# The up-projection's moving operand is read from its last column to its first, and its tiles are laid out 4128 bytes apart

## The chip, the cores and the metric

The kernel runs on one core of a Trainium2 chip. A core has a matrix engine (TensorE, PE in the profile, with its weight loads as PEld), a vector engine (VectorE, DVE), a scalar engine (ScalarE, ACT), a general engine (GpSimd, POOL) and an engine that here only issues DMAs (SyncE, SP). SBUF is the working memory of 128 partitions, PSUM holds the matmul results in eight banks. Times are device microseconds of one execution. The kernel before takes 2546.99 us, the median of 2 runs (2546.63 and 2547.34).

## The reference

```python
x = A_x                                               # 2 x 1 x 4096 x 640
g = _sigmoid((x * gate_w).sum(-1, keepdims=True))
a = _A_ref(x, A_w1, A_b1, A_w2, A_b2)
b = _B_ref(x, B_w_gate, B_w_up, B_w_down)
return g * a + (1 - g) * b

# _B_ref: (gelu(x @ w_gate) * (x @ w_up)) @ w_down, with 640 -> 1728 -> 640
# _A_ref: rfft over the 4096 tokens; in four blocks of 160 channels a complex two-layer MLP
#         (relu between), soft threshold at 0.01; irfft
```

There are 8192 tokens of 640 channels. The largest part is branch B, two projections of 640 to 1728 columns (w_gate and w_up, together the "up-projection" here) and one back.

## The kernel before, in words

All matrix products are built from a high and a low part. A float32 operand is split into a rounded part (ScalarE, `high`, L276) and the rest (VectorE, `low`, L279), both of type float32r, and a product is three matmuls: high times high, high times low, low times high. Each matmul has one weight load (LDWEIGHTS) of 128 columns of its own, so PE and PEld have equal counts.

The kernel has three stages:

1. The up-projection, from the start to about 1388 us. It goes through 16 blocks of 512 tokens, three times, once for each of three groups of hidden columns. The hidden layer h is written to DRAM (`h_store`). Beside it, ScalarE, VectorE and a few matmuls (L619) compute the gate and the first step of the Fourier transform.
2. The spectral MLP of branch A, to about 1812 us: the second step of the transform (L783), two layers (L295, L860 to L863), the first step back.
3. The down-projection together with the last step of the inverse transform, to the end.

In stage 1 the tokens are the moving operand (tiles xo, 256 tokens a matmul, streamed through the array) and the projection weights the stationary one (tiles w0 to w3). `quad` multiplies two 2x2 blocked matrices with seven products instead of eight, so the tokens enter as sums and differences of blocks, named b11, b21, b12, b22, k4 and t1 to t5. Each name is one tile xo of [128 partitions, 2 parts, 512 tokens]; t5 holds 256 tokens. `x_of` cuts from these tiles the pieces of 256 columns that the matmuls read. A quad runs 54 matmuls in seven runs: of 9, 9, 6, 9, 9, 6 and 6, each run over one tile or two. `plain` (first block of the first group) runs 60 matmuls without the seven-product form, `mixed` (the last 64 gate and 64 up columns, once a block in the third group) 30. All matmuls of this stage and of the down-projection are issued in `run`, so they stand under one line, L472, and are told apart by their tiles: xo and w here, wx and ho in the down-projection.

The tiles xo come from the pool tag "mid", which has 14 slots, each as large as the largest mid tile. The other users of mid are of the later stages (z, zz, zl, h, hs, s2s and the down-projection's wx in part). Before the first mid tile the helper `mid` allocates two small tiles named gap and clears them on POOL (L239): one in a "tiny" slot, one of 112 words in a tag of its own, which sets where the mid slots begin. As the program is built, the mid slots stand at 171,712 + 4096k bytes within each partition, so each starts 64 bytes past a multiple of 128. The tiles of the other pools that TensorE reads (w0, w1, w2 and ho in "big", w3 in "tiny", xs in "small") start at multiples of 128.

The tokens reach xo in two ways. In the first group each xo is made from the raw tokens (xraw, loaded by SP from in_xT), and t1 to t4 are also written to DRAM (xD, by POOL's queue). In the other groups t1 to t4 are loaded back ready split, 124 loads by SP's queue. Nothing is put in order by a planner: the program writes each engine's order out by hand (hooks at numbered points of each quad, and lists of due loads).

The host lays out the inputs before the launch: `_layouts` permutes and reshapes, among them the array xT from which xraw is loaded.

Of the kernel before, what the change touches and what calls it, by code (L numbers as in the profile page):

```python
# [10 lines left out]
F32 = mybir.dt.float32  # L11
# [4 lines left out]
P = 128  # L16
# [134 lines left out]
def _tokens():  # L151

    n2, q = np.arange(32)[:, None], NB[None, :]
    return np.where(n2 < 16, 32 * q + n2, 32 * (P - 1 - q) + n2)


def _layouts(a):

    A = lambda n: np.asarray(a[n])
    c = np.ascontiguousarray  # L160
    x = A("A_x")[:, 0]
    even, odd = np.arange(BS), np.roll(np.arange(BS), -32)
    main = np.concatenate([n * BS + (odd if n % 2 else even)[:P] for n in range(NBLK)])
    rest = np.concatenate([n * BS + (odd if n % 2 else even)[P:] for n in range(NBLK)])
    perm = np.concatenate([main, rest])
    xt = x[:, _tokens()]
    o = {"x": c(xt[..., perm]), "gate": c(A("gate_w")[perm][None])}

    xp = xt.reshape(16, 2, 256, 5, P).transpose(0, 4, 1, 3, 2)
    o["xT"] = c(np.stack([xp[:, :, 0, :2], xp[:, :, 0, 2:4], xp[:, :, 1, :2], xp[:, :, 1, 2:4], xp[:, :, :, 4]],  # L170
                         axis=1).reshape(16, 5, P, 512))

    g, u = A("B_w_gate"), A("B_w_up")
    cols = []
    for t in range(NPAIR):
        cols += [g[:, t * P:(t + 1) * P], u[:, t * P:(t + 1) * P]]
    cols.append(np.concatenate([g[:, NPAIR * P:], u[:, NPAIR * P:]], axis=1))
    o["wgu"] = c(np.stack([m.reshape(5, P, P).transpose(1, 0, 2) for m in cols]))
    o["wd"] = c(A("B_w_down"))

    w1, w2 = A("A_w1"), A("A_w2")
    w1 = np.stack([w1[:, n][:, odd if n % 2 else even] for n in range(NBLK)], axis=1)
    b1, b2 = A("A_b1")[:, :, None], A("A_b2")[:, :, None]

    def wide1(w):
        m, r = w[..., :P], w[..., P:]
        return np.concatenate([m[1], r[1], r[0], r[1], m[0], m[1]], axis=-1)

    def wide2(w):
        return np.concatenate([w[1], w[0], w[1]], axis=-1)  # L190

    def long1(w):
        m, r = w[..., :P], w[..., P:]
        return np.concatenate([m[0], m[1], r[0], r[1]], axis=-1)

    def long2(w):
        return np.concatenate([w[0], w[1]], axis=-1)

    def rows(w, f, order):
        return np.stack([f(w[[z, 1 - z], :, i]) for z, i in order])  # L200
    i32 = range(P, BS)
    tr = lambda w: c(w.transpose(1, 0, 2))
    o["w1m"], o["w2m"] = tr(wide1(w1[:, :, :P])), tr(wide2(w2[:, :, :P]))
    o["w1l"] = c(rows(w1, long1, [(z, i) for i in i32 for h in range(2) for z in range(2)]))
    o["w2l"] = c(rows(w2, long2, [(z, i) for h in range(2) for z in range(2) for i in i32]))
    o["w1s"] = c(np.concatenate([rows(w1, long1, [(z, i) for i in i32 for z in range(2)]),
                                 tr(long1(b1)).repeat(2, 0)]))
    o["w2s"] = c(np.concatenate([rows(w2, long2, [(z, i) for z in range(2) for i in i32]),
                                 tr(long2(b2)).repeat(2, 0)]))
    return o  # L210
# [3 lines left out]
def spectral_mix_kernel(ctx: ExitStack, tc: tile.TileContext, a):  # L214
# [7 lines left out]
    pool = ctx.enter_context(tc.tile_pool(name="pool", bufs=1))  # L222
# [7 lines left out]
    gap = []  # L230
# [3 lines left out]

    def mid(shape, dt=F32, name="mid"):
        if not gap:
            gap.extend([tiny([P, 1], name="gap"), pool.tile([P, 112], F32, name="gap", tag="gap", bufs=1)])
            for t in gap:
                nc.gpsimd.memset(t, 0.0)  # L239
        return pool.tile(shape, dt, name=name, tag="mid", bufs=14)  # L240
# [4 lines left out]
    def tiny(shape, dt=F32, name="tiny"):  # L245
        return pool.tile(shape, dt, name=name, tag="tiny", bufs=15)
# [168 lines left out]
    def x_prep(key, k, eng=nc.vector):  # L415
# [4 lines left out]
        def src():  # L420
            d = XT[key]
            if not made(key) and kept is not None:
                m = mid([P, 2, 512], F32R, name="xo")
                ld(m.rearrange("p h n -> p (h n)").bitcast(F32), xD[key[1]][:, kept])
                XO.setdefault(key, {})[name] = [m[:, h] for h in range(2)]
                return
            for n, p, q in (("t1", "b12", "b11"), ("t2", "b22", "t1"), ("t3", "b22", "b12"), ("t4", "b21", "t2")):
                if n not in d and (n == name or (n, name) == ("t1", "t2")):
                    d[n] = small([P, 512], name="xd")
                    nc.vector.tensor_sub(d[n], d[p], d[q])  # L430
            if name == "t5":
                d[name] = small([P, 256], name="xd")
                nc.vector.tensor_sub(d[name], d["k4"][:, :256], d["k4"][:, 256:])
            return d[name]

        def hi():
            if not made(key) and kept is not None:
                return
            if name == "t5":
                if not T5:  # L440
                    T5.append(mid([P, 2, 2, 256], F32R, name="xo"))
                t = [T5[0][:, keys.index(key) % 2, h] for h in range(2)]
            else:
                m = mid([P, 2, 512], F32R, name="xo")
                t = [m[:, h] for h in range(2)]
                if kept is not None:
                    XM[key, name] = m
            XO.setdefault(key, {})[name] = t
            high(t[0], XT[key][name])
# [30 lines left out]
    def x_of(o, *names):  # L480

        tiles = []
        for n in names:
            n, q = n if isinstance(n, tuple) else (n, None)
            h, l = o[n]
            for k in ((0,) if n == "t5" else (0, 1) if q is None else (q,)):
                tiles.append((h[:, 256 * k:256 * k + 256], l[:, 256 * k:256 * k + 256]))
        return tiles

    Q = []  # L490
# [1 line left out]
    def quad(key, t, hook):  # L492
# [8 lines left out]

        X = half()
        run(X, prod(w["g1"], x_of(o, "b11", ("k4", 0))))
        p1 = T("p1")
        copy(p1, X)
        hook(0)
        old[0]()
        hook(1)
        C = half()
        run(C, prod(w["s3"], x_of(o, "t3", ("k4", 1))))  # L510
        hook(2)
        A = half()
        run(A, prod(w["g2"], x_of(o, "b21")))
        nc.vector.tensor_add(p1, A, p1)  # L514
        hook(3)
# [961 lines left out]
```

## Time and profile before

| | before |
|---|---|
| median of the runs | 2546.99 us |
| lowest and highest run | 2546.63, 2547.34 us |
| profiled execution, first to last instruction (span) | 2546.4 us |
| TensorE busy | 2535.1 us of the span |
| weight loads busy | 2530.4 us |
| VectorE, ScalarE, GpSimd busy | 2055.1, 1502.8, 370.2 us |
| instructions | 54296 |

The profiled execution's span ends 0.6 us under the median of the runs. In a row of a group, the name left of the arrow is what is written and those right of it are what is read, then come the shape and the count; behind the first bar the group's busy time in us and the mean length of one instruction in ns; behind the second the engine's idle time ahead of it and whom it waited for. Matmuls overlap each other in the array, so their mean length is longer than the distance at which they follow each other. That distance comes from the chain of work that ended last, listed in order of time: each row is a start, a length (both in us) and a count of instructions that followed each other without a gap.

### The profile page before, as it was taken

The numbers are of one execution on the slowest core, as the hardware profiler recorded it, in microseconds if no ns is written. First come the engines' busy times: TensorE is split into PE (matmuls) and PEld (weight loads), VectorE is DVE, ScalarE is ACT, GpSimd is POOL, SyncE is SP. The second block draws the span as 40 slices with busy tenths as digits, with TensorE's granted clock in tenths as the row PEclk, the third lists the DMA queues.
The fourth block names the chain that finished last, engine by engine and source line by source line (L and its number), as shares of the span: only waits on it lengthen the run. The fifth ranks groups of instructions, "written<-read, shape, count | busy, mean of one in ns | idle before, by whom it ended". The sixth has DMA issues, their size and how long they took to land.

```text
span 2546.4 us, 54296 instructions
## 1 busy us (share of the span) xinstructions
PE 2535.1 (100%) x20276; PEld 2530.4 (99%) x20276; DVE 2055.1 (81%) x4212; ACT 1502.8 (59%) x3490; POOL 370.2 (15%) x370
## 2 busy tenths in 40 slices
PE   9999999999999999999999999999999999999999
PEld 9999999999999999999999999999999999999999
DVE  7778777777777766776667788888899999999998
ACT  6555555666665655555556777778644444445443
POOL 0000000000000000000002111111133333333332
PEclk9999999999999999999999999999999999999999
DMA  6565657676767667776667455548844444344442
GB/s 232 190 215 196 212 170 234 205 236 211 219 205 249 207 213 231 224 230 214 212 222 223 129 153 150 160 137 266 291 149 138 150 156 158 120 144 156 155 136 92
DMA packets 346060, 483.48 MB, mean 190 GB/s; under 512 B 24701, under 2 KB 222717, under 8 KB 345797
## 3 DMA queue, kind: packets, MB, share of 16 engines
q1 hardware_dynamic: 331108, 438.47, 54.5%
q0 software_dynamic: 14688, 41.56, 4.5%
q8 instruction: 159, 2.61, 0.4%
q14 instruction: 105, 0.85, 0.1%
HBM read 300.29 MB, written 179.64 MB: 188 GB/s over the span
## 4 chain that ended last, share of the span: by engine, by line
PE 97%; DMA 1%; DVE 1%; issue 0%; ACT 0%; SPq 0%; DVEq 0%; ACTq 0%
PE bank L472 77%; PE bank L295 14%; PE bank L783 3%; PE bank L619 1%; DMA wx<-wdf 1%; PE bank L861 1%; PE bank L860 1%; DMA wx<-wdl 0%; PE bank L863 0%; DVE xo L279 0%; DMA wraw<-in_wgu_dram 0%; DVE xd L430 0%; DVE h L543 0%; DVE w L279 0%; DVE wl L715 0%
## 5 line engine op out<-in xcount | busy, mean ns | idle before, releaser
L472 PE MATMUL bank<-xo,w 128*128 128x256 f32 x11736 | 1362.0, 277 | 6.3 <-ACT xo L276 5.1
L472 PEld LDWEIGHTS bank<-xo,w 128*128 128x128 f32 x11736 | 1353.0, 188 | 7.5 <-ACT xo L276 5.1
L472 PE MATMUL bank<-wx,ho 128*128 128x320 f32 x4608 | 678.6, 308 | 0.1
L472 PEld LDWEIGHTS bank<-wx,ho 128*128 128x128 f32 x4608 | 674.1, 188 | 0.6 <-DMA wx<-wdf 0.3
L498 ACT ACTIVATE u<-bank 128x256 f32<-128x256 f32 x408 | 156.7, 384 | 258.0 <-PE bank L472 252.5
L279 DVE TENSOR_TENSOR ho<-hraw,ho 128x640 fp32r<-128x640 f32 (+3 forms) x384 | 276.9, 761 | 5.0 <-ACT ho L276 3.0
L276 ACT ACTIVATE ho<-hraw 128x640 fp32r<-128x640 f32 x320 | 166.3, 574 | 64.1 <-PE bank L472 46.8
L498 ACT ACTIVATE p<-bank 128x256 f32<-128x256 f32 x204 | 78.6, 385 | 149.0 <-PE bank L472 66.4
L279 DVE TENSOR_TENSOR xo<-xraw,xo 128x512 fp32r<-128x512 f32 x209 | 142.9, 684 | 25.2 <-ACT xo L276 24.7
L531 DVE TENSOR_TENSOR u<-bank,u 128x256 f32<-128x256 f32 x204 | 85.9, 421 | 90.8 <-ACT u L498 88.2
L279 DVE TENSOR_TENSOR xs<-xr,xs 64x640 fp32r<-64x640 f32 x128 | 105.0, 820 | 58.0 <-ACT xs L276 56.0
L1165 ACT ACTIVATE uu<-bank,gs 128x320 f32<-128x320 f32 x120 | 55.0, 525 | 160.0 <-PE bank L295 157.7
L295 PE MATMUL bank<-wm,h 128*128 128x320 f32 (+1 forms) x792 | 137.8, 309 | 0.0
L540 DVE TENSOR_TENSOR u<-bank,u 128x256 f32<-128x256 f32 x204 | 85.5, 419 | 62.2 <-PE bank L472 61.3
L276 ACT ACTIVATE xo<-xraw 128x512 fp32r<-128x512 f32 x209 | 131.0, 627 | 7.1 <-DMA xraw<-in_xT_dram 5.3
L621 DVE TENSOR_TENSOR as<-bank,as 64x320 f32<-64x320 f32 x256 | 113.9, 484 | 25.0 <-ACT as L620 24.0
L295 PEld LDWEIGHTS bank<-wm,h 128*128 128x128 f32 (+1 forms) x792 | 118.6, 185 | 1.2
L276 ACT ACTIVATE ho<-hs 128x640 fp32r<-128x640 f32 (+1 forms) x128 | 71.9, 576 | 77.8 <-PE bank L472 57.7
L572 POOL MEMSET h<- 64x512 f32 x16 | 8.4, 522 | 747.7 <-PE bank L619 369.4
L514 DVE TENSOR_TENSOR p<-bank,p 128x256 f32<-128x256 f32 x204 | 86.5, 424 | 36.6 <-PE bank L472 32.2
L279 DVE TENSOR_TENSOR s2s<-s,s2s 128x320 fp32r<-128x320 f32 x128 | 111.6, 929 | 0.9 <-ACT s2s L276 0.9
L620 ACT ACTIVATE as<-bank 64x320 f32<-64x320 f32 x256 | 96.8, 427 | 16.5 <-PE bank L619 14.0
(157 smaller groups left out, 3470.7 us busy)
## 6 DMA issues: line engine op xcount, KB each, us to landing
xo<-xD SPq DMA_DIRECT2D x124, 512.0 KB
xraw<-in_xT_dram SPq DMA_DIRECT2D x225, 256.0 KB
hD<-h SPq DMA_DIRECT2D x224, 256.0 KB
hraw<-hD SPq DMA_DIRECT2D x128, 320.0 KB
xD<-xo POOLq DMA_DIRECT2D x64, 512.0 KB, 4.4
sc<-scr SPq DMA_DIRECT2D x65, 320.0 KB
xr<-in_x_dram SPq DMA_DIRECT2D x64, 320.0 KB
scr<-as SPq DMA_DIRECT2D x64, 320.0 KB
```

What stands on the lines that cost most here:

```text
L276: nc.scalar.activation(dst, src, AF.Copy, scale=scale)
L279: eng.tensor_sub(dst, src, hi.bitcast(F32))
L295: nc.tensor.matmul(dst, l, r, start=i == 0, stop=i == len(ops) - 1)
L472: nc.tensor.matmul(dst, l, r, start=first and i == 0, stop=i == len(ops) - 1, skip_group_check=True)
L498: copy = lambda d, s_: nc.scalar.activation(d, s_, AF.Copy)
L514: nc.vector.tensor_add(p1, A, p1)
L531: nc.vector.tensor_add(u4, C, u4)
L540: nc.vector.tensor_add(u2, C, u2)
L620: nc.scalar.activation(stg[hi, cs], pa[lo, :320], AF.Copy)
L621: nc.vector.tensor_add(stg[hi, cs], pa[hi, :320], stg[hi, cs])
L783: nc.tensor.matmul(pz[:, kp * P:(kp + 1) * P], SC[b, c, kp][:, o:o + P], ft, start=True, stop=True)
L1165: nc.scalar.activation(uu[n2][:, cs], pe[:, :320], AF.Copy, scale=gs[:, b, 0, n2:n2 + 1])
```

## The change

Three edits. On the host, the last axis of the array behind xT, the 256 tokens of a half block, is turned round. In `x_of`, both parts of each piece of 256 columns are handed to the matmul with step -1, from the last column to the first; the product in PSUM therefore has the order of before. In `mid`, the gap tile of 112 words in its own tag becomes one of 1032 words in the tag mid; since 1032 words are more than any other mid tile has (1024), the slots become 4128 bytes long. As the program is built they stand at 171,264 + 4128k, that is 0, 32, 64, 96, 0, ... bytes past a multiple of 128, fourteen different starts modulo 4096. The whole of the memory used is the same, and so is the order of the instructions on PE, DVE, ACT and SP; on POOL one memset is longer. Two tiles, the split of an xd and one load of xo, now also carry a wait for POOL's memset, as the first users of the slot after the gap tile.

```diff
@@ _layouts
-    xp = xt.reshape(16, 2, 256, 5, P).transpose(0, 4, 1, 3, 2)
+    xp = xt.reshape(16, 2, 256, 5, P).transpose(0, 4, 1, 3, 2)[..., ::-1]
@@ mid
-            gap.extend([tiny([P, 1], name="gap"), pool.tile([P, 112], F32, name="gap", tag="gap", bufs=1)])
+            gap.extend([tiny([P, 1], name="gap"), pool.tile([P, 1032], F32, name="gap", tag="mid", bufs=14)])
             for t in gap:
                 nc.gpsimd.memset(t, 0.0)
@@ x_of
-                tiles.append((h[:, 256 * k:256 * k + 256], l[:, 256 * k:256 * k + 256]))
+                tiles.append(tuple(x[:, 256 * k:256 * k + 256][:, ::-1] for x in (h, l)))
```

## The prediction

> **What bounds the kernel now.** I read the page's busy line first, then the granted clock, then the chain that ended last, and last the groups by line and shape. The clock comes from the view of cores, the rest from the page and from the list of groups of TensorE.
>
> ```profile
> span 2546.4 us, 54296 instructions
> PE 2535.1 (100%) x20276; PEld 2530.4 (99%) x20276; DVE 2055.1 (81%) x4212; ACT 1502.8 (59%) x3490; POOL 370.2 (15%) x370
> q1 hardware_dynamic: 331108, 438.47, 54.5%
> PE 97%; DMA 1%; DVE 1%; issue 0%; ACT 0%; SPq 0%; DVEq 0%; ACTq 0%
> ```
>
> ```profile
> core 0: 2546.4 us, clock 1.000
> L472 PE MATMUL bank<-xo,w 128*128 128x256 f32 x11736 | 1362.0, 277 | 6.3 <-ACT xo L276 5.1 <-ACT u L498 0.9 <-DVE xo L279 0.4
> L472 PE MATMUL bank<-wx,ho 128*128 128x320 f32 x4608 | 678.6, 308 | 0.1
> L295 PE MATMUL bank<-z,wm 128*128 128x256 f32 x360 | 62.2, 281 | 0.0
> L239 POOL MEMSET gap<- x2: 99/146/192, 0.7 to 0.8; 128x1 f32 x1, 128x112 f32 x1
> ```
>
> TensorE ends last for 97% of the span, and for the up-projection (the 11,736 matmuls that read xo) it stood idle 6.3 us in all. So the time is the number of matmuls times the spacing at which they start. The mean of 277 ns is the length of one pipelined matmul and not that spacing. The spacing is seen in the chain listed in order of time, in which an unbroken run of matmuls is one row (start, length, count):
>
> ```profile
> 6.03 3.67 PE bank L472 x16
> ...
> 66.91 22.38 PE bank L472 x190
> 89.29 0.29 PE bank L619 x2
> ```
>
> ```profile
> 243.56 21.56 PE bank L472 x190
> 290.22 0.29 PE bank L619 x2
> 290.51 2.97 PE bank L472 x26
> 293.77 74.95 PE bank L472 x661
> 1352.21 0.89 PE bank L783 x8
> 1858.52 21.02 PE bank L472 x144
> ```
>
> Four things are to be seen. (a) The long undisturbed row gives 74.95/661 = 113.4 ns for one matmul of 256 columns. (b) The same work with the same tiles ran in another rhythm at 66.9 us: 22.38/190 = 117.8 ns, 4.4 ns more each, through the whole row. The shapes and the pools it reads from are the same, so the spacing isn't fixed by the column count alone. (c) L619 reads a tile of another pool (xs), which starts at a multiple of 128 bytes, while every xo tile of before starts 64 bytes past one (the built program puts the mid slots at 171,712 + 4096k). After those two matmuls the next row is dearer: 2.97 us for 26 where 26 x 113.4 ns = 2.95, so 22 ns more; and 21.56 us for 190 where 21.54 is due, 16 ns more. A visit to a tile of another class and back costs the next few matmuls about 19 ns, then the old rhythm returns. (d) At 128 columns a row of L783 takes 0.89/8 = 111 ns a matmul, hardly less than at 256 columns: there the weight load, one for each matmul, sets the pace.
>
> **The change, part by part.** No instruction is added, removed or moved on PE, DVE, ACT or SP; the order by engine is the same in both programs. Three things change.
>
> First, the gap tile of 112 words in its own slot becomes one of 1032 words in a mid slot. The one clearing instruction that grows on POOL took at most 192 ns for 112 words; nine times that is 1.7 us, and by its row POOL had begun it at 0.8 us. Its only followers are a split on ACT and one xo load in SP's queue that reuse this slot some thirteen mid tiles later; the memset is over long before. Cost 0. If a wait did go to it, it would be once, under 2 us.
>
> Second, the widest mid tile is now 4128 bytes instead of 4096, so the fourteen slots lie 4128 apart, from 171,264 on: 0, 32, 64 or 96 bytes past a multiple of 128 in turn (four, four, three and three slots). Before, all fourteen were alike. The pool takes 14 x 32 = 448 = 112 x 4 bytes more and the gap gives those back; every other pool stays where it was.
>
> Third, each of the 11,736 matmuls of the up-projection reads its 256 columns with step -1 from offset 255. The host has reversed the tokens, so the products and PSUM are as before, and the splits and DMAs still write forward. What DVE, ACT and DMA do has slack: ACT 59% busy, DVE 81%, the hardware queue 54.5% of the engines' time. That the 124 loads of xo now land on 32-byte starts is therefore hidden unless they become so slow that TensorE, which waited 6.3 us in all, begins to wait for them.
>
> What the step of -1 costs has no row: no matmul of before reads backwards. The bounds per matmul:
> - below nothing: down to the 111.3 ns of L783, -2.1 ns, 11,736 x -2.1 = -25 us;
> - nothing: the rhythm of 113.4 ns holds, 0;
> - the other rhythm, 117.8 ns: 11,736 x 4.4 = 52 us;
> - far above: columns streamed at half the rate. The row at 6.03 us, the kernel's first matmuls, which ran at about half the later pace, stands nearest: 3.67/16 = 229 ns, +116 ns each, 11,736 x 116 = +1,360 us.
>
> [...]
>
> I take the step itself at nothing, and price the classes. The nearest row for those is (c), a tile of another class. One quadruple product runs 54 matmuls over 11 xo tiles in turn (seven runs, four of them over two tiles); 204 of those, 4 plain blocks with 12 turns each and 16 mixed ones with 6 make 204 x 11 + 48 + 96 = 2,388 changes of tile. Before, none changed class. Now two different slots share a class with chance (4x3 + 4x3 + 3x2 + 3x2)/(14x13) = 0.20, so about 1,910 changes do. At 19 ns each: 36 us. For bounds: 0 if only the direction relative to the weights counts, and 2,388 x 22 ns = 53 us if all pay the dearer price. A step of 32 bytes has no row; I price it as the one of 64.
>
> The other readers of mid slots still read forward: the z matmuls (62.2 us), a few groups of its kind, and some 960 of the 4,608 down-projection matmuls, whose weights lie in mid slots. The row of these is 21.02/144 = 146.0 ns; 320 columns at the pace of (a) would be 141.7. So +/-4.3 ns on 960 is +/-4 us, and as much again for the z groups: 0 taken, +/-8 us kept.
>
> Sum against the profiled execution: 2546.4 + 36 = 2582.4 us of span. The median of the runs is 0.6 us above that span, so 2583 us, 1.4% slower. A measurement of this kernel can tell 2% (51 us) from no change: the borders are 2496 and 2598.
>
> **The rivals.**
>
> *The change is invisible* (it doesn't do what it says, as far as time goes): the spacing stays at 113.4 ns and the time at 2540 to 2555. For it: (a) holds for 661 matmuls that go through many tiles, at distances of many slots. Against it: (b) and (c), the same matmul at two spacings.
> [...]
>
> *A better rhythm.* Reading backwards pairs differently with the weight load, and the spacing falls to the load's own pace of 111.3 ns: -25 us, 2521. For it: that pace exists. Against it: 113.4 was reached with all tiles in one class, and now four classes must all lock. It can't gain 2%, as the load floor stops it.
>
> *A worse rhythm, on the slow side.* Place: each start of a moving stream in the up-projection. Mechanism: with changing classes the good rhythm of (a) never re-forms and everything runs as in (b), 52 us, while each change of class still pays, 36 us: 2546.4 + 88 = 2634. It decides from 117.8 ns on average: more than 51 us over 11,736 matmuls is 4.4 ns each. If half of all matmuls paid the 22 ns of (c), 129 us, it would be 2675. For it: row (b) shows that a rhythm once lost can stay lost for 190 matmuls. Against: in all later rows it came back after a few.
>
> *The stream runs at half rate backwards:* +1,360 us, 3,900. [...] Then ACT and DVE would idle before PSUM results, and nothing else would move.
>
> **How the numbers follow.** Forecast (classes cost, the direction doesn't), 2555 to 2597: 0.44. Invisible, 2540 to 2555: 0.13. Better rhythm, 2515 to 2540: 0.07. Worse rhythm, 2597 to 2680: 0.19, of it 0.18 past 2598. Half rate, about 3,900: 0.14. Anything else, 0.03: 0.02 faster than 2496, 0.01 between 2680 and 3,900. The range from 2515 to 2680 leaves out 0.17. Faster by over 2%: 0.02; within 2%: 0.44 + 0.13 + 0.07 + 0.01 = 0.65; slower: 0.18 + 0.14 + 0.01 = 0.33. Within the forecast's own case the time is 2555 to 2597.
>
> **What the profile of the changed kernel would show.** If I am right, the chain's long rows of L472 stand at 115.5 to 117 ns a matmul (76.3 to 77.3 us for the row of 661), with no row as clean as 113.4; the group of xo matmuls is busy some 1,398 us; the rows of L619 and the two stages behind the up-projection keep their length within 10 us. Half rate shows at once as 2,700 us busy in that group. The invisible case keeps the row of 661 at 74.95. The worse rhythm shows rows near 120 ns. I am wrong in kind if xo matmuls begin to wait for loads (their idle time far above 6.3 us), or if the down-projection, which still reads forward, takes the difference.

## The result and the profile after

The changed kernel takes 2604.14 us, the median of 2 runs (2603.86 and 2604.41), against 2546.99 us: the ratio is 1.0218 with a 95% interval from 1.0201 to 1.0234, so it is 2.2% slower.

First lines of the changed kernel's page, then the gap tile's row from the view of its line, and the clock from the view of cores.

```profile
span 2602.1 us, 54297 instructions
PE 2590.7 (100%) x20276; PEld 2586.6 (99%) x20276; DVE 2062.6 (79%) x4212; ACT 1505.0 (58%) x3490; POOL 374.0 (14%) x370
...
L472 PE MATMUL bank<-xo,w 128*128 128x256 f32 x11736 | 1414.6, 282 | 6.2 <-ACT xo L276 5.2
L472 PE MATMUL bank<-wx,ho 128*128 128x320 f32 x4608 | 680.0, 309 | 0.3 <-DVE ho L279 0.3
L239 POOL MEMSET gap<- x2: 99/528/958, 0.7 to 0.8; 128x1 f32 x1, 128x1032 f32 x1
core 0: 2602.1 us, clock 1.000
```

The span grew by 55.7 us, and the xo matmuls are busy 1414.6 us instead of 1362.0, 52.6 us more. Their idle time is 6.2 us against 6.3: no new wait for loads or splits came up. The clock is the same. The memset of the gap tile takes 0.96 us and holds nobody up.

Where the time went in the stages is read from the first and last start of the two groups under L472. The view of that line gives them, of before and then of after (duration as minimum, median and maximum in ns, then first and last start in us):

```profile
L472 PE MATMUL bank<-xo,w x11736: 276/276/583, 5.1 to 1386.3; 128*128 128x256 f32 x199
L472 PE MATMUL bank<-wx,ho x4608: 302/309/414, 1812.1 to 2541.6; 128*128 128x320 f32 x192
```

```profile
L472 PE MATMUL bank<-xo,w x11736: 278/282/582, 5.2 to 1438.5; 128*128 128x256 f32 x199
L472 PE MATMUL bank<-wx,ho x4608: 302/309/417, 1865.8 to 2597.3; 128*128 128x320 f32 x192
```

The up-projection ends 52.2 us later. The MLP stage between (1812.1 - 1386.3 = 425.8 us before, 1865.8 - 1438.5 = 427.3 after) grew by 1.5 us and the last stage by 2.0 us. So the loss is in the matmuls that the change touches. The chain in order of time shows at which spacing:

```profile
226.44 22.53 PE bank L472 x190
248.98 0.29 PE bank L619 x2
249.27 3.07 PE bank L472 x26
...
305.02 150.58 PE bank L472 x1270
...
1935.33 21.09 PE bank L472 x144
```

The longest run gives 150.58/1270 = 118.6 ns a matmul, the row of 190 the same, where before has 113.4. No long row comes near the old spacing, and there is nothing special behind the L619 pairs any more: 3.07/26 = 118.1 ns. The rhythm of 113.4 ns is gone everywhere, not only where a tile changes. The down-projection's row is 21.09 us against 21.02.

### The profile page after: what moved, and what is told of

Its sections match the earlier page's. It is cut to its first block, busy times and chain, and to the rows that moved or that the text cites. A ratio compares the mean times of both kernels' runs of the same rounds, so it can differ in the third digit from the quotient of the medians.

```text
span 2602.1 us, 54297 instructions
## 1 busy us (share of the span) xinstructions
PE 2590.7 (100%) x20276; PEld 2586.6 (99%) x20276; DVE 2062.6 (79%) x4212; ACT 1505.0 (58%) x3490; POOL 374.0 (14%) x370
## 4 chain that ended last, share of the span: by engine, by line
PE 97%; DMA 1%; DVE 1%; ACT 1%; issue 0%; SPq 0%; POOL 0%; ACTq 0%; DVEq 0%; POOLq 0%
PE bank L472 78%; PE bank L295 14%; PE bank L783 3%; PE bank L619 1%; PE bank L861 1%; PE bank L860 1%; DMA s<-scr 0%; PE bank L863 0%; DMA wx<-wdf 0%; DMA hraw<-hD 0%; DMA zl<-zl 0%; DVE ho L279 0%; DMA xraw<-in_xT_dram 0%; POOL hs L1116 0%; ACT ho L276 0%
## 5 line engine op out<-in xcount | busy, mean ns | idle before, releaser
L472 PE MATMUL bank<-xo,w 128*128 128x256 f32 x11736 | 1414.6, 282 | 6.2 <-ACT xo L276 5.2
L472 PEld LDWEIGHTS bank<-xo,w 128*128 128x128 f32 x11736 | 1404.9, 188 | 7.1 <-ACT xo L276 5.2
L472 PE MATMUL bank<-wx,ho 128*128 128x320 f32 x4608 | 680.0, 309 | 0.3 <-DVE ho L279 0.3
L472 PEld LDWEIGHTS bank<-wx,ho 128*128 128x128 f32 x4608 | 675.8, 188 | 0.6 <-DVE ho L279 0.6
```

The source lines that it names most:

```text
L472: nc.tensor.matmul(dst, l, r, start=first and i == 0, stop=i == len(ops) - 1, skip_group_check=True)
```

## The experiments

The theories after the result were three: the reading direction spoils the rhythm; the mixed slots spoil it; or what counts is how the place of a moving tile stands to that of the weights, and direction and slot act together. "D" is the start of an xo tile minus the start of a weight tile in bytes, modulo 512, as the built program places them; before has D = 448 for every tile, the changed kernel fourteen values from 0 to 416 in steps of 32. Each ratio is against runs of the kernel before taken beside it, whose medians lie between 2546.86 and 2548.19 us.

### Direction alone and slots alone

The changed kernel with the slots of before (D = 448):

```diff
-            gap.extend([tiny([P, 1], name="gap"), pool.tile([P, 1032], F32, name="gap", tag="mid", bufs=14)])
+            gap.extend([tiny([P, 1], name="gap"), pool.tile([P, 112], F32, name="gap", tag="gap", bufs=1)])
```

> Reads backwards, with the slots of before (all 64 bytes past a multiple of 128). If the reading direction alone spoils the rhythm: 2600 us, the xo matmuls start 118 to 119 ns apart. If the mixed slots alone do it: 2547 us and 113.4 ns. If direction and slot act together (a backward stream from a slot at 64 meets the weight load as a forward stream from a slot at 0 does): about 2600 us here too, and the two runs with uniform slots at 0 tell this from the first.

Measured: 2592.26 us, ratio 1.0167 (1.0152 to 1.0182).

The kernel before with the slots of the changed kernel, reading forward:

```diff
-            gap.extend([tiny([P, 1], name="gap"), pool.tile([P, 112], F32, name="gap", tag="gap", bufs=1)])
+            gap.extend([tiny([P, 1], name="gap"), pool.tile([P, 1032], F32, name="gap", tag="mid", bufs=14)])
```

> Reads forward, with the slots of the changed kernel (0, 32, 64 and 96 past a multiple of 128). If direction alone: 2547 us, 113.4 ns. If the mixed slots alone: about 2600 us, 118 to 119 ns. If both act together: between, about 2575 us, with tiles at 64 still near 113 ns and tiles at 0 near 118 ns.

Measured: 2597.83 us, ratio 1.0189 (1.0172 to 1.0206). The chain in order of time, of the first kernel and then of the second:

```profile
225.20 22.38 PE bank L472 x190
...
303.28 149.74 PE bank L472 x1270
```

```profile
199.70 22.28 PE bank L472 x190
...
303.59 150.07 PE bank L472 x1270
```

Each half of the change alone costs nearly as much as both; either is under 2%, but its interval is clear of no change. Backward reading in the old slots runs at 149.74/1270 = 117.9 ns, forward reading in the new slots at 118.2. The two costs, 1.7% and 1.9%, don't add up to 3.6%: there is one good rhythm to be lost, and either half loses it. Neither theory of a single cause stands.

### All slots alike, but in another place

Forward with a gap of 96 words (D = 384), and backward with the same gap:

```diff
-            gap.extend([tiny([P, 1], name="gap"), pool.tile([P, 112], F32, name="gap", tag="gap", bufs=1)])
+            gap.extend([tiny([P, 1], name="gap"), pool.tile([P, 96], F32, name="gap", tag="gap", bufs=1)])
```

> Reads forward, all slots alike but at multiples of 128 (gap of 96 words in place of 112). If direction alone: 2547 us, as before. If it is the mixing of slots that costs: 2547 us too. If the place of a slot against the weights' matters: about 2600 us, one steady spacing of 118 ns or more.

Measured: 2607.11 us, ratio 1.0227 (1.0211 to 1.0242).

> Reads backwards, all slots alike at multiples of 128. If direction alone: 2600 us. If mixing alone: 2547 us. If direction and slot act together, a backward stream from a slot at 0 is the mirror of a forward one from a slot at 64: 2547 us, 113.4 ns.

Measured: 2621.41 us, ratio 1.0282 (1.0266 to 1.0297). Chain rows, forward and then backward:

```profile
225.96 22.55 PE bank L472 x190
```

```profile
228.71 22.80 PE bank L472 x190
```

Here every tile stands alike and no change of class occurs, yet forward runs at 118.7 ns, slower than the mixed slots, and backward at 120.0. So the loss needs no mixing; the place is enough. The mirror idea fell too: backward from multiples of 128 is the worst of all runs, not the equal of forward from 64 past one.

### Whose place: the tile's own, or against the weights

A pad of 64 bytes ahead of all pools moves the weights and, with the gap of 112 words, the xo tiles alike (D stays 448, xo now at multiples of 128). The second kernel has the pad and a gap of 96 words: both 64 past a multiple of 128, D = 384.

```diff
+    pad = consts.tile([P, 16], F32, name="pad")
+    nc.gpsimd.memset(pad, 0.0)
     fny = consts.tile([P, 8], F32, name="fny")
```

> Forward. A pad of 64 bytes ahead of all pools puts the weights 64 past a multiple of 128 and the xo tiles at multiples of 128: both moved, their difference is that of before. If the difference between moving tile and weights sets the rhythm: 2547 us, 113.4 ns. If the moving tile's own place does: 2605 us, 118.7 ns, as with xo at 0 and the weights at 0.

Measured: 2548.23 us, ratio 0.9998 (0.9988 to 1.0007).

> Forward. Weights and xo tiles both 64 past a multiple of 128. If the difference sets the rhythm: 2605 us, 118.7 ns, as with both at 0. If the moving tile's own place does: 2547 us, 113.4 ns.

Measured: 2607.71 us, ratio 1.0231 (1.0216 to 1.0247). Chain rows of the first and of the second (the pad moves the line of `run` to L474):

```profile
217.41 21.56 PE bank L474 x190
239.25 2.97 PE bank L474 x26
...
292.73 74.95 PE bank L474 x661
```

```profile
226.16 22.55 PE bank L474 x190
```

The first repeats before to the last digit (21.56 and 74.95 us), the second the forward run at D = 384 (22.55). The difference between the two addresses decides, not where either lies. That is the clearest result of the study. The pad moves the small pool too, so this pair alone doesn't say that the weights are the partner; the last run below moves the small pool by itself.

### Which differences

Forward with gaps of 104, 80 and 48 words (D = 416, 320 and 192), the same line as above with the other number:

> Forward, weights at 0, all xo tiles 32 past a multiple of 128. If 64 is the only good place of the four: 2590 to 2610 us. If the spacing goes over from good to bad step by step: about 2575 us, 116 ns.

Measured: 2604.48 us, ratio 1.0219 (1.0204 to 1.0235).

> Forward, weights at 0, xo tiles 64 past a multiple of 128 as before, but 128 bytes lower (gap of 80 words). If the place modulo 128 is what counts: 2547 us, 113.4 ns. If a longer period counts (256 or 512): 2590 to 2610 us.

Measured: 2593.14 us, ratio 1.0171 (1.0156 to 1.0186).

> Forward, gap of 48 words: xo tiles start 192 bytes past the weights modulo 512, where before has 448, the run with the gap of 80 words 320 and the run at 0 has 384. If the difference counts modulo 256: 2547 us, 113.4 ns. If it counts modulo 512 or more: about 2590 us, 117.8 ns, as at 320.

Measured: 2547.75 us, ratio 1.0002 (0.9993 to 1.0012). Chain rows of the three in this order:

```profile
225.10 22.55 PE bank L472 x190
...
251.28 22.29 PE bank L472 x190
```

```profile
224.42 22.38 PE bank L472 x190
```

```profile
218.76 21.56 PE bank L472 x190
```

D = 192 is as good as 448, and 320 isn't, though all three are 64 modulo 128. So the period is 256 bytes as far as these runs go, and of the forward differences tried the good one is 192 modulo 256. The theory that the place modulo 128 counts fell, and so did that of a spacing that goes over step by step: 416, only 32 bytes from 448, costs about as much as 384. At 416 there are two kinds of rows, two of the nine at 22.55 us and seven at 22.29 or 22.30 (117.3 ns). One of the fourteen mixed slots stands at 192. In the forward run with mixed slots, by the trace's start times and the built places, the matmuls on that slot follow each other at 116.6 ns on average, those on the other thirteen at 117.2 to 119.2: the good place shows there too, but its rhythm doesn't settle.

Does a backward stream have a good difference of its own? The changed kernel's read with gaps of 120 and 116 words (D = 480 and 464):

> Backwards, all xo tiles 480 past the weights modulo 512 (gap of 120 words), the one step of 32 bytes that neither the changed kernel nor the other backward runs hold. If a backward stream has a good difference of its own among the steps of 32: about 2547 us, 113.4 ns, here. If it has none: 2590 to 2620 us.

Measured: 2595.94 us, ratio 1.0193 (1.0179 to 1.0207).

> Backwards, all xo tiles 464 past the weights modulo 512 (gap of 116 words): a step of 16 bytes, half the grid that the other runs hold. If a backward stream has a good difference between the steps of 32 (and only there): about 2547 us, 113.4 ns. If direction alone is enough to keep the good rhythm away: 2590 to 2620 us, as at 448 and 480.

Measured: 2596.14 us, ratio 1.0187 (1.0170 to 1.0204). Chain rows of both:

```profile
224.64 22.38 PE bank L472 x190
```

```profile
225.41 22.38 PE bank L472 x190
```

None found. With the mixed slots of the changed kernel, which hold every step of 32 from 0 to 416, and the uniform runs at 384, 448, 464 and 480, no long backward row comes under 117.7 ns. A row of the changed kernel runs over many slots; taken slot by slot its matmuls follow each other at 117.8 to 119.3 ns, and none stands out as 192 does forward. Of steps finer than 32 bytes only the one at 464 was tried.

### A version that might beat both

If D = 192 modulo 256 were good for 320 columns too, the matmuls of L619 and the down-projection would gain. A pad of 48 words ahead of the small pool, one of 16 words between the small and the big pool and a gap of 48 words set the small pool off the big one, so that the tiles of L619 and some of the down-projection's stand at 192 or 448 modulo 512 instead of 0 or 256, and keep xo at D = 192:

```diff
+    pad = consts.tile([P, 48], F32, name="pad")
...
     def big(shape, dt=F32, name="big"):
+        if not gap2:
+            gap2.append(pool.tile([P, 16], F32, name="gap2", tag="gap2", bufs=1))
...
-            gap.extend([tiny([P, 1], name="gap"), pool.tile([P, 112], F32, name="gap", tag="gap", bufs=1)])
+            gap.extend([tiny([P, 1], name="gap"), pool.tile([P, 48], F32, name="gap", tag="gap", bufs=1)])
```

> Forward, xo tiles at 192 past the weights as in the run before it, and besides the small pool moved by 192 bytes against the big one, so that the xs tiles against f1, and the down-projection's wx pieces that lie in small slots against ho, stand 192 or 448 past them instead of 0 or 256. If the good difference serves the matmuls of 320 columns too: the two L619 matmuls at 140 ns each instead of 147 and no slow matmuls behind them, some 4 us, and a part of the 768 moved pieces at 140 instead of 147, some 3 to 5 us: 2538 to 2541 us. If it is bound to 256 columns: 2547 us. If 192 is no good difference: about 2590 us.

Measured: 2549.09 us, ratio 1.0007 (0.9998 to 1.0016). Its chain rows, with L619 now at L624:

```profile
240.76 0.29 PE bank L624 x2
241.05 2.96 PE bank L477 x26
...
1882.32 21.01 PE bank L477 x144
```

The L619 pairs still take 0.29 us and the down-projection's row 21.01 us against 21.02, so the fall to 140 ns a matmul that was expected of a good difference didn't come, and no version faster than before came out of this. A small gain hides under the rows' two digits: by the start times, the mean of the 128 pairs is 291.7 ns against 295.4, and the xo matmuls behind a pair lose 11 ns instead of 20 before the rhythm is back. That is under 2 us in all, less than these medians can tell. The run also shows that the place of the small pool isn't what sets the rhythm of the xo matmuls: their row of 26 takes 2.96 us with the small pool elsewhere. The weights are left as the partner, since they are the other operand that these matmuls read; the tiny pool, which kept its distance to the weights' big pool in every run, wasn't told apart from them.

## Why the prediction was right and where it was wrong

The measured 2604 us lie in the range from 2515 to 2680 and on the side that was forecast, but 6 us past the border of 2598. The forecast's own case, 2555 to 2597, didn't happen; what the rival "a worse rhythm" described did, at a chance of 0.19, and its price of 88 us was too high by half: 57 us were measured. That the forecast came within 21 us of the result is luck: its 36 us stood for a toll that isn't what costs here, and what does cost was put at nothing.

- **What bounds the kernel** held. TensorE's spacing is the time; 52.2 of the 55.7 us of span are in the up-projection, and no other engine or queue became the limit. The cost of 0 for the gap tile, for the 32-byte starts of the loads and the order on the queues held: the xo matmuls' idle time is 6.2 us.
- **"I take the step itself at nothing" was wrong.** Alone, in the slots of before, it costs 1.67%, 45.2 us of group busy time (1407.2 against 1362.0):

```profile
L472 PE MATMUL bank<-xo,w 128*128 128x256 f32 x11736 | 1407.2, 281 | 6.2 <-ACT xo L276 5.3 <-ACT u L498 0.6 <-DVE xo L279 0.2
```

  That is the bound which row (b) of the prediction gave: 117.8 ns, read at 66.9 us of before, is to the digit the row of all uniform backward runs but the one at 384 (22.38/190). The bound was right and the choice within it wrong. No run shows the 0 that the sum has for the step: with the slots of before the step cost 4.4 ns a matmul (117.8 against 113.4).
- **The price per change of class was the wrong mechanism.** I charged 19 ns at 1,910 changes, 36 us. The new slots alone, read forward, cost more, 1410.3 - 1362.0 = 48.3 us of busy time:

```profile
L472 PE MATMUL bank<-xo,w 128*128 128x256 f32 x11736 | 1410.3, 281 | 5.9 <-ACT xo L276 5.1 <-ACT u L498 0.5 <-DVE xo L279 0.2
```

  And a kernel without any change of class, forward at 384, costs 2.27%. The size read from (c) was right: by the start times the matmuls behind an L619 pair lose 20 ns in before. But (c) showed a rhythm that is lost and found again within a few matmuls, with all xo tiles at a good difference; I took the cost of losing it once for the price of any move between classes. Where the tiles stand at a bad difference no long row shows 113.4 ns; read forward at 320, 384 and 416, the long rows lie between 117.3 and 118.7. For this the row would have had to be read as "which difference brings the rhythm back", not as a toll.
- **"0 if only the direction relative to the weights counts"** named the right pair, stream against weights, but as a reason for no cost. It is the distance within this pair that decides, and the change took thirteen of the fourteen xo slots off the good ones; the one that it put at 192 gains nothing, as it is read backward (117.8 ns a matmul).
- **The rivals.** "Invisible" is refuted by the 2604 us, and the padded pair of runs, 2548 and 2608 us with nothing changed but the place of the xo tiles against the rest, speaks against it too. "Better rhythm" didn't occur. Its floor, the load's pace in (d), is seen in before at 4 columns too: four loads for L783 (matmuls of 128 columns) start at 1389.81 us, the four for L797 (4 columns) at 1390.26 and the next for L783 at 1390.70: 112 and 110 ns a load. "Half rate" didn't occur: the slowest backward row, at 384, runs at 120.0 ns (22.80/190). "Worse rhythm" was right in the place and in what happens, a good rhythm that never forms again, but not in its reason, the changing classes: the backward run in the old slots and the forward run at 384 lose it without any. Mis-sized was its sum, which added 36 us for changes of class to 52 us for the lost rhythm. The 52 us alone fit what the xo group shows (52.6), in part by luck: the mean spacing of xo matmuls went from 114.4 to 118.8 ns, so before was a little slower than its 113.4 and the changed kernel slower than the 117.8 of (b).
- **The classes of the other stages** were priced at 0 with 8 us kept on either side: 3.5 us (1.5 and 2.0).

## What to carry to other kernels

When matmuls with a weight load each run back to back, read their spacing from long undisturbed rows of the chain and not from the mean length (113.4 ns and 277 ns in before). If the same shape shows two spacings in one trace, as 113.4 and 117.8 ns in before, the better one may hang on the layout and can be lost, here for 57 us: before moving a pool or turning a stream, work out the distance between the moving tile and the weights and keep it. Try a layout as uniform distances, one run each; a mixture shows little but the loss (2597.83 us read forward, with one of its slots at 192).

## What the runs showed of the hardware that was not expected

- For 256 fp32r columns with a weight load each, the spacing is 113.4 ns where the moving tile starts 192 or 448 bytes past the weights modulo 512, and 117.3 to 118.7 ns at 320, 384 and 416, read forward (long rows). It depends on the difference: moving both operands by 64 bytes changed nothing (2548 us), moving one cost 2.3%.
- Read backward, no difference tried gave less than 117.7 ns in a long row, and the worst, 120.0 ns, was at 384. That is far from half rate: the worst row is 6.6 ns above the best forward spacing.
- 117.8 ns recurs as a rhythm of its own: at 66.9 us in before, at the good difference, and as the same 22.38 us in the forward run at 320 and three backward runs. Before has left it in its next row of 190, as its chain shows:

```profile
92.94 21.54 PE bank L472 x190
```

  So a good difference allows the rhythm of 113.4 ns but doesn't force it from the first matmul on. Why both rhythms occur at one difference, and why the difference counts at all, isn't settled by these runs.
- For 320 columns no difference with a like gain was found: the down-projection's spacing stayed at 146 ns (21.01/144) with part of the tiles at 192. It isn't blind to the place either: with its tiles in mid at other differences its row took between 21.00 us (the run at 320) and 21.13 (at 384).
